# The filter of a spectral layer in another SBUF layout, and four more buffers for row results

## Chip, core and metric

The kernel runs on one core of one Trainium2 chip. The metric is the device time of one execution in microseconds. Before the change three runs took 368.7, 370.02 and 371.12 us, so the median is 370.02 us.

## What is computed

A layer in two halves, its output, and the gradients of its inputs:

```python
def _A_ref(x, w_r, w_i):                       # x: 2048 x 448
    X = rfft2(x.astype(float32), axes=(-2, -1))  # 2048 x 225, complex
    X = X * (w_r + 1j * w_i)                     # the filter: two planes of 2048 x 225, bf16
    return irfft2(X, s=(S, D), axes=(-2, -1)).astype(bfloat16)

def _B_ref(x, w1, b1, w2, b2):
    h = _layernorm(x, axis=-1)
    u = gelu(einsum("bsd,sf->bdf", h, w1) + b1)  # f = 1792
    y = einsum("bdf,fs->bds", u, w2) + b2
    return y.transpose(0, 2, 1)

h  = x + _A_ref(_layernorm(x), A_w_r, A_w_i)
h2 = h + _B_ref(_layernorm(h), B_w1, B_b1, B_w2, B_b2)
# returned: h2, and the gradients for x, A_w_r, A_w_i, w1, b1, w2, b2 under grad_out
```

All inputs and outputs are bf16. The gradients of A_w_r and A_w_i have the shape of the filter, 2048 x 225 each.

## The kernel before

The Fourier transform of the 448 columns and of the 2048 rows is done with matmuls. The 2048 rows are split into 16 x 128.

**Forward rows** (up to 45 us). For each of 16 groups of 128 rows, `row_a` and `row_b` make a short transform along the rows and the transform along the columns on TensorE (PE). `row_b` evicts its result from PSUM into a buffer of `cs_ring`; when both halves of a buffer are full, `defer` plans a reshuffle: a DMA on the queue of SyncE (SP) from the buffer, SBUF to SBUF, into `D2` (region r2). There are eight such reshuffles (line 669) and, before the change, four buffers in region r452, so the fifth to eighth buffer fill waits until an earlier reshuffle has read its buffer.

**Beside it.** While the row groups run, `fill(n)` puts matmuls of another product in between: 14 blocks of 16 matmuls that need w2 transposed. `load_w2T` (line 306) loads those blocks with DMA transposes on the SP queue. The filter is loaded in the same loop: `w_io` is a generator that issues one DMA per step, and `W_AT` says how many steps each of the 16 loop turns takes. Tables of sines that the mixing needs (`Ut`, `Vt`, from `base` and `gen_UV`) are made on VectorE (DVE), GpSimd (POOL) and ScalarE (ACT) at the same time.

**Mixing** (`s2_stage`, forward from 61 us). Four sets of four groups. For each set, small 32 x 32 matmuls (`four`, line 223) on `D2` finish the row transform; the results are evicted to `x`, which is `Xs` in region rX; `w_mult` multiplies by the filter on DVE in complex arithmetic, two groups at a time: two large products (128 x 904) and two sums (128 x 452) each. Then `four` again mixes back, and 32 more reshuffles (line 698) bring the result to `D3`. Between the sets `fill` puts in the other product's matmuls. `inv_rows` then finishes the inverse transform.

**The rest.** From 117 us on come the two large products of the second half, and then the gradients. The backward pass repeats rows, mixing and inverse rows. In its mixing (264 to 318 us) `bwd_mult` does `w_mult`, and then with `Xs` the gradient of the filter, which overwrites the filter in region rW. The inverse rows of the backward pass (from 318 us) are woven with matmuls of the weight gradients. `w_io` issues the filter's gradients as stores there, in the turns that `GW_AT` names.

**What sets the order.** PE, DVE, ACT and SP keep the order in which the program issues the work. Evictions go to ACT or DVE: `evac` compares two running sums of estimated costs, and `Meter.slack` limits how far the sums may drift apart (2.0, in the backward mixing 10.0). `defer` puts a DMA into SP's order at a planned time after PE's matmuls.

**The filter's layout.** Region rW holds `W` as [128 partitions, 16 groups, 2 planes, 226]; 225 columns are used, the last is set to zero. Partition 32i + c*16 + l (i, c, l from 0 to 3, 1 and 15) holds row 16i + g + 128l for c = 0, and the mirrored row 128 - 16i - g + 128l for c = 1; g is the group. The loads go per plane and per i: one move for c = 0, one for c = 1, and one for a single row that falls out of the pattern. That makes 18 moves, each to 16 neighbouring partitions, in runs of 450 bytes:

```python
for p0, g0, g1, row, dims in ((0, 0, 16, 16 * i, [[DF, 16], [1, DF]]),
                              (16, 0 if i else 1, 16, 128 - 16 * i - (not i), [[-DF, 16 if i else 15], [1, DF]]),
                              (16, 0, 1, 64, [[1, DF]])):
```

Of the kernel before, what the change touches and what calls it, by code (L numbers as in the profile page):

```python
# [12 lines left out]
I32 = mybir.dt.int32  # L13
ALU = mybir.AluOpType
# [108 lines left out]
def kernel(  # L123
# [339 lines left out]
    def gen_UV():  # L463
        i_, c_, s_ = decode(gp_)
        nrow, i16, z, mk, k0, k1, ou, ov0, ov1, pu, pv = (col() for _ in range(11))
        gp_madd(nrow, c_, 16.0, s_)
        gp_.tensor_scalar(out=i16, in0=i_, scalar1=16.0, scalar2=None, op0=ALU.mult)
        gp_.tensor_scalar(out=z, in0=i_, scalar1=0.0, scalar2=None, op0=ALU.is_equal)
        gp_.tensor_tensor(out=mk, in0=z, in1=c_, op=ALU.mult)
        gp_.tensor_scalar(out=k1, in0=mk, scalar1=-1.0, scalar2=1.0, op0=ALU.mult, op1=ALU.add)  # L470
        gp_.tensor_tensor(out=k0, in0=k1, in1=z, op=ALU.add)
        gp_.tensor_scalar(out=k0, in0=k0, scalar1=-1.0, scalar2=2.0, op0=ALU.mult, op1=ALU.add)
        gp_.tensor_scalar(out=ou, in0=c_, scalar1=1536.0, scalar2=1536.0, op0=ALU.mult, op1=ALU.add)
        gp_.tensor_scalar(out=ov0, in0=c_, scalar1=-512.0, scalar2=2048.0, op0=ALU.mult, op1=ALU.add)
        gp_.tensor_scalar(out=ov1, in0=ov0, scalar1=1024.0, scalar2=None, op0=ALU.add)
        for pt, o, kk in ((pu, ou, -1536.0), (pv, ov1, -512.0)):
            gp_.tensor_scalar(out=pt, in0=s_, scalar1=64.0, scalar2=kk, op0=ALU.mult, op1=ALU.add)
            gp_madd(pt, pt, mk, o)
        yield
        ve.tensor_scalar(out=permI[:], in0=krow[:, 0:32], scalar1=nrow, scalar2=None, op0=ALU.is_equal)  # L480
        ve.scalar_tensor_tensor(out=base[:, 0, 1, :], in0=fix, scalar=mk, in1=base[:, 0, 1, :], op0=ALU.mult, op1=ALU.add)
        bi = base.bitcast(I32)
        ve.tensor_scalar(out=bi, in0=base, scalar1=i16, scalar2=None, op0=ALU.add)
        ve.tensor_scalar(out=bi, in0=bi, scalar1=2047 - 64, scalar2=None, op0=ALU.bitwise_and)
        yield
        for dst, o0, o1, pt in ((Ut, ou, ou, pu), (Vt, ov0, ov1, pv)):
            t = ftmp(1024 if dst is Ut else 2048, 16, 2, 16).bitcast(I32)
            for k, o in ((0, o0), (1, o1)):
                ve.tensor_scalar(out=t[:, :, k, :], in0=bi[:, :, k, :], scalar1=s_, scalar2=o, op0=ALU.mult, op1=ALU.add)
                yield  # L490
            ve.tensor_scalar(out=t[:, 0, 1, :], in0=bi[:, 0, 1, :], scalar1=s_, scalar2=pt, op0=ALU.mult, op1=ALU.add)
# [3 lines left out]
            sc.activation(out=dst[:].rearrange("p g m -> p (g m)"), in_=t.rearrange("p g k l -> p (g k l)"), func=ACT.Sin,  # L495
                          scale=s2048, bias=half_uv)
            yield True
            for c, k in ((1, k0), (0, k1)):
                v = dst[:, 0, 16 * c:16 * c + 16]
# [55 lines left out]

    W = cut(rW, 0, NG, 2, KW)

    def w_io(dr, di, store):  # L560
        for c_, d in ((0, dr), (1, di)):
            for i in range(4):
                for p0, g0, g1, row, dims in ((0, 0, 16, 16 * i, [[DF, 16], [1, DF]]),
                                              (16, 0 if i else 1, 16, 128 - 16 * i - (not i), [[-DF, 16 if i else 15], [1, DF]]),
                                              (16, 0, 1, 64, [[1, DF]])):
                    if i and row == 64 and g1 == 1:
                        continue
                    p0 += 32 * i
                    sb = W[p0:p0 + 16, g0:g1, c_, 0:DF]
                    d_ap = bass.AP(d.tensor, d.offset + row * DF, [[P * DF, 16]] + dims)  # L570
                    nc.sync.dma_start(out=d_ap if store else sb, in_=sb if store else d_ap)  # L571
                    yield

    r452_ring = ring(r452, 0, 8, 2, KW)
    Xs = cut(rX, 0, NG, 2, KW)
# [2 lines left out]
    Y_ring = ring(rS, 1808, 2, 4, 2, KW)  # L578
    aT_ring = ring(rAT, 0, 2, 4, P)
    D2 = cut(r2, 0, NG, 2, KW)  # L580
    cs_ring = ring(r452, 0, 4, 2, 2, KW)
    D3 = cut(r3, 0, NT, 2, KW)

    _ei = [0]

    def resh_eng():
        _ei[0] += 1
        return nc.sync

    def rowbase(s_):  # L590
        return 32 * (s_ // 4) + s_ % 4
# [54 lines left out]
    def row_b(h, quarters=False):  # L646
# [19 lines left out]
        else:  # L666
            evac(out=cs[:, c], in_=pv)
        if c:
            defer(RESH_LAG, lambda: nc.sync.dma_start(out=D2[u:u + 125:4, 8 * e:8 * e + 8].rearrange("p g c k -> p (g c k)"),
                                                      in_=cs.rearrange("p x c k -> p (x c k)")), cs)  # L670

    def s2_stage(get_x, on_mult, n1, n2, gap, after=None, scale=None):
# [15 lines left out]
        for s in range(5):  # L688
            if s < 4:
                x = get_x(s)  # L690
                for a, pv in enumerate(four((Vt, Ut, Un), s, 1, lambda a, g, r: D2[blk(r), g])):
                    evac(out=x[:, a], in_=pv, scale=scale)
            fill(n1)
            if s:
                for g, pv in zip(set_groups(s - 1), four((VTt, UTt, UTn), s - 1, -1, lambda a, g, r: y[blk(r), a])):
                    ab = r452_ring.next()
                    evac(out=ab, in_=pv)
                    defer(RESH_LAG, lambda g=g, ab=ab: nc.sync.dma_start(out=D3[rowbase(g):rowbase(g) + 29:4, :, :, :], in_=ab), ab)
# [10 lines left out]
        ve.tensor_scalar(out=dst, in0=src, scalar1=-1.0, scalar2=None, op0=ALU.mult)  # L709

    def w_mult(xc, w, y, conj):
        wr = w[:, :, 0:1, :].broadcast_to([P, 2, 2, KW])
        wi = w[:, :, 1:2, :].broadcast_to([P, 2, 2, KW])
        p1, p2 = p_ring.next(), p_ring.next()
        ve.tensor_tensor(out=p1, in0=xc, in1=wr, op=ALU.mult)
        ve.tensor_tensor(out=p2, in0=xc, in1=wi, op=ALU.mult)
        ve.tensor_tensor(out=y[:, :, 1, :], in0=p1[:, :, 0, :], in1=p2[:, :, 1, :],
# [103 lines left out]
    base = ftmp(3072, 16, 2, 16)  # L821
    fix = ftmp(3584, 16)
    pcolb = col()
    ve.tensor_copy(out=pcolb, in_=pcol)
    nc.vector.memset(base[:, 0, 0, 0:1], 0.0)
    nc.vector.memset(base[:, 0, 1, 0:1], 0.0)
    for k in range(2):
        gp_.iota(base.rearrange("p (e a c) k l -> p k e a c l", e=2, a=4)[:, k],
                 pattern=[[8, 2], [18, 4], [1, 2], [128 - 256 * k, 16]], base=1920 * k,
                 channel_multiplier=0, allow_small_or_imprecise_dtypes=True)  # L830
    gp_.iota(fix, pattern=[[256, 16]], base=-1920, channel_multiplier=0, allow_small_or_imprecise_dtypes=True)
# [380 lines left out]


    def bwd_mult(s, j, xc, y):
        xs = set_of(Xs, s)[:, 2 * j:2 * j + 2]
        gw = set_of(W, s)[:, 2 * j:2 * j + 2]
        w_mult(xc, gw, y, True)
        p1, p2 = p_ring.next(), p_ring.next()
        ve.tensor_tensor(out=p1, in0=xc, in1=xs[:, :, 0:1, :].broadcast_to([P, 2, 2, KW]), op=ALU.mult)
        ve.tensor_tensor(out=p2, in0=xc, in1=xs[:, :, 1:2, :].broadcast_to([P, 2, 2, KW]), op=ALU.mult)  # L1220
        ve.tensor_tensor(out=gw[:, :, 0, :], in0=p1[:, :, 0, :], in1=p2[:, :, 1, :], op=ALU.add)
        ve.tensor_tensor(out=gw[:, :, 1, :], in0=p1[:, :, 1, :], in1=p2[:, :, 0, :], op=ALU.subtract)

# [65 lines left out]
            fill(8)  # L1289
        rows(t)  # L1290
    fill(N_FILL_B[2])
    Meter.slack = 10.0
    s2_stage(lambda s: X_ring.next(), bwd_mult, 14, 22, N_FILL_B[4], {1: lambda: load_du(0), 3: lambda: load_du(2)},
             2.0 * INV_SD)
    Meter.slack = 2.0
    g_out = w_io(out_2, out_3, True)
    X_AT = {0: 2, 4: 3}
    GW_AT = tuple(range(14)) + (1, 3, 5, 7)

    def gx_consumer(t, py):  # L1300
        if t in X_AT:
# [90 lines left out]
```

## Time and profile before

The profiled execution took 368.8 us; its span, from the first to the last instruction, is 367.0 us.

| | busy us | share of the span |
|---|---|---|
| PE, matmuls | 334.0 | 91% |
| PEld, weight loads (beside PE) | 174.7 | 48% |
| DVE | 248.2 | 68% |
| ACT | 198.3 | 54% |
| POOL | 69.0 | 19% |
| SP's DMA queue, share of 16 engines | | 87.2% |

| stretch, us | what runs | PE busy, us | DMA, GB/s |
|---|---|---|---|
| 0 to 21 | loads, tables | 14.5 of 21.0 | 250 |
| 21 to 45.6 | forward rows, filter loads | 23.0 of 24.6 | 166 |
| 45.6 to 61.1 | up to the first mixing matmul | 3.3 of 15.5 | 158 |
| 61.1 to 98.2 | forward mixing | 35.3 of 37.1 | 170 |
| 98.2 to 117.2 | inverse rows | 18.3 of 19.0 | 241 |
| 117.2 to 264.7 | large products, backward rows | 145.3 of 147.5 | 210 |
| 264.7 to 318 | backward mixing | 51.5 of 53.3 | 233 |
| 318 to 367 | inverse rows, weight gradients, stores | 42.8 of 49.0 | 244 |

How to read the views: the slices cut the span into 40 equal parts of 9.2 us, each digit is a busy share in tenths, and PEclk is the clock that was granted to PE. The chain of waits follows the work back from the last instruction, in order of time, as start, length and what; `SPq` is an instruction that issues a DMA, and `DMA a<-b` the time until such a move arrived. The waits list an engine, the line and tile, and what ended its idle time. In the groups of instructions each line has the operation, the tiles, the shape, the count, the busy time and the mean time of one in ns, and the idle time before. Names such as `r` stand for regions whose number is left out. Line 82 is a helper through which all DVE and ACT work goes, and line 218 the one through which most matmuls go.

### The profile page before, as it was taken

The page shows a single profiled execution, that of the slowest core. Times are in us where ns is not written, and L with a number is a line of the kernel's source. Part 1 is how long each engine was busy: PE and PEld are TensorE (multiplying, and loading weights), DVE is VectorE, ACT ScalarE, POOL GpSimd, SP SyncE. Part 2 cuts the span into 40 slices and gives each one's busy share as a digit, 9 for nine tenths or more (in the row PEclk, how much of TensorE's full clock was granted, in tenths as well). Part 3 has the DMA queues.
Part 4 walks back from the last instruction along what each step waited for, and adds up shares of the span by engine and source line. Part 5 has one row for each costly group of instructions (what it writes and reads, how often), then busy time and mean ns, then how long its engine had stood idle before and what let it go on. Part 6 is the DMA issues. An engine that isn't in the chain of part 4 may idle for free.

```text
span 367.0 us, 7798 instructions
## 1 busy us (share of the span) xinstructions
PE 334.0 (91%) x2810; PEld 174.7 (48%) x2819; DVE 248.2 (68%) x662; ACT 198.3 (54%) x436; POOL 69.0 (19%) x220
## 2 busy tenths in 40 slices
PE   8769833998999999999999999999898999999993
PEld 3346511444564555555555555554333434456551
DVE  8896323685188488859423788887389585479993
ACT  5466331364298645451321245557358887479972
POOL 5766000000022000000100111110000000047981
PEclk9989965999999999999999999999999999999999
DMA  8999999656994899967786898855986698999987
GB/s 222 275 191 162 178 146 181 150 122 167 263 319 167 284 327 290 261 164 211 208 195 159 176 204 162 194 93 138 293 267 192 206 242 232 225 282 239 212 242 262
DMA packets 151087, 78.03 MB, mean 213 GB/s; under 512 B 99784, under 2 KB 144072, under 8 KB 150920
## 3 DMA queue, kind: packets, MB, share of 16 engines
q1 hardware_dynamic: 150760, 77.13, 87.2%
q8 instruction: 22, 0.36, 0.4%
q10 hardware_dynamic: 288, 0.39, 0.3%
q14 instruction: 17, 0.14, 0.1%
HBM read 25.71 MB, written 22.04 MB: 130 GB/s over the span
## 4 chain that ended last, share of the span: by engine, by line
PE 72%; DVE 7%; DMA 6%; SPq 5%; ACT 5%; issue 2%; DVEq 0%; POOL 0%; ACTq 0%
PE ps_mm L218 62%; PE ps_ff L218 8%; DVE r L82 3%; DMA r<-r 3%; PE ps_ff L223 3%; SPq L306 3%; ACT rO L82 2%; DVE rS L82 2%; DMA rW<-in_A_w_i_dram 2%; DMA rA<-in_A_x_dram 1%; ACT r L82 1%; DVE rA L82 1%; SPq L316 1%; ACT rX L82 0%; SPq L571 0%
## 5 line engine op out<-in xcount | busy, mean ns | idle before, releaser
L218 PEld LDWEIGHTS <-r 128*128 128x128 bf16 (+2 forms) x600 | 56.0, 105 | 44.9 <-issue 2.3
L218 PEld LDWEIGHTS <-rS 128*128 128x128 bf16 (+2 forms) x496 | 40.3, 98 | 40.7 <-issue 8.1
L218 PE MATMUL ps_mm<-rD,r 128*128 128x448 bf16 x224 | 44.5, 352 | 0.0
L82 ACT CAST rO<-ps_mm 128x512 bf16<-128x512 f32 (+1 forms) x67 | 35.9, 586 | 13.3 <-PE ps_mm L218 8.8
L218 PEld LDWEIGHTS <-rst 128*128 128x128 bf16 (+1 forms) x320 | 23.4, 97 | 31.5 <-issue 14.6
L218 PE MATMUL ps_mm<-rC,rE 128*128 128x448 bf16 x144 | 34.9, 382 | 1.1 <-DMA rC<-in_grad_out_dram 1.0
L82 ACT CAST r<-ps_ff 128x452 bf16<-128x452 f32 x47 | 25.6, 585 | 18.5 <-DMA r<-r 10.8
L218 PE MATMUL ps_mm<-rB,r 128*128 128x448 bf16 x160 | 31.2, 352 | 0.1
L218 PE MATMUL ps_mm<-rG,rst 128*128 128x512 bf16 (+1 forms) x122 | 26.7, 380 | 0.9 <-ACT rO L82 0.4
L218 PE MATMUL ps_mm<-r,rst 128*128 128x512 bf16 (+2 forms) x144 | 27.2, 345 | 0.2 <-ACT rG L82 0.2
L82 DVE CAST r<-ps_ff 128x452 bf16<-128x452 f32 x17 | 10.4, 634 | 21.1 <-DMA r<-r 13.2
L82 ACT ACTIVATE r<-ps_mm,rstd_h 128x448 bf16<-128x448 f32 x16 | 10.2, 635 | 26.8 <-PE ps_mm L218 26.8
L82 DVE SCALAR_TENSOR_TENSOR r<-ps_mm,b2col,r 128x448 bf16<-128x448 f32 x16 | 10.9, 683 | 19.9 <-PE ps_mm L218 17.2
L82 ACT ACTIVATE r<-rC 128x448 bf16<-128x448 bf16 x16 | 9.1, 572 | 26.6 <-DMA out_dram<-r 18.7
L218 PE MATMUL ps_mm<-rE,rS 128*128 128x448 bf16 x112 | 21.5, 352 | 0.0
L82 ACT ACTIVATE rG<-rG 128x896 bf16<-128x896 bf16 x14 | 13.3, 951 | 14.9 <-DVE rG L82 14.7
L218 PEld LDWEIGHTS <-rO 128*128 128x128 bf16 (+1 forms) x165 | 15.2, 98 | 12.3 <-ACT rO L82 0.2
L82 ACT CAST rS<-ps_ff 128x512 bf16<-128x512 f32 x31 | 17.9, 582 | 5.0 <-PE ps_ff L218 4.9
L1137 POOL TENSOR_SCALAR lcol<-lcol 128x1 f32<-128x1 f32 x16 | 8.5, 530 | 64.7 <-ACT r L82 64.7
L218 PEld LDWEIGHTS <-rE 128*128 128x128 bf16 x144 | 14.3, 104 | 12.9 <-issue 4.4
L82 ACT CAST rG<-ps_mm 128x512 bf16<-128x512 f32 (+1 forms) x34 | 16.7, 543 | 6.7 <-PE ps_mm L218 6.4
L218 PE MATMUL ps_ff<-csI,rAT 113*128 113x224 bf16 (+1 forms) x108 | 19.0, 298 | 0.6 <-ACT rAT L82 0.4
(191 smaller groups left out, 604.5 us busy)
## 6 DMA issues: line engine op xcount, KB each, us to landing
out_dram<-rO SPq DMA_DIRECT2D x34, 256.0 KB
r<-in_B_w_dram SPq DMA_DIRECT2D x5, 1024.0 KB
r<-r SPq DMA_DIRECT2D x16, 226.0 KB
r<-r SPq DMA_DIRECT2D x32, 113.0 KB
rS<-in_B_w_dram SPq DMA_DIRECT2D x4, 896.0 KB
out_dram<-rG SPq DMA_DIRECT2D x10, 256.0 KB
rO<-in_B_w_dram SPq DMA_DIRECT2D x2, 1024.0 KB
rC<-in_grad_out_dram SPq DMA_DIRECT2D x4, 448.0 KB
```

The costliest lines, as they stand in the source:

```text
L82: fn(**kw)
L218: nc.tensor.matmul(out, lhsT=lhsT, rhs=rhs, start=start, stop=stop)
L223: nc.tensor.matmul(out, lhsT=lhsT, rhs=rhs, start=start, stop=stop)
L306: nc.sync.dma_start_transpose(out=wT, in_=B_w2[j * P:(j + 1) * P, :].rearrange("f (t c) -> f t c", c=P))
L316: nc.sync.dma_start(out=go_tp[:, 4 * q:4 * q + 4, :], in_=go_tp_d[:, 4 * q:4 * q + 4, :])
L1137: gp_.tensor_scalar(out=m1, in0=ms, scalar1=-1.0 / D, scalar2=None, op0=ALU.mult)
```

## The change

The filter is kept plane by plane: [128 partitions, 2 planes, 16 groups, 225], without the padding column. The two kinds of rows now alternate over the partitions: partition 32i + 2l + c instead of 32i + 16c + l. In an even partition the 16 groups of a plane are then one run of 7200 bytes in SBUF and in memory, and one move brings all 64 even partitions of a plane. The mirrored rows stay runs of 450 bytes, 16 partitions per move, but these lie two apart, over 32. Loads and stores go from 18 to 12 moves each. The tables `Ut` and `Vt` follow the new order of partitions, so their intermediate steps are made with another stride. DVE's products take 225 columns instead of 226. `cs_ring` gets four more buffers, in region rX, for the forward rows alone. The filter's moves are issued in other loop turns, and `Meter.slack` in the backward mixing goes from 10.0 to 7.0.

```diff
-        ve.scalar_tensor_tensor(out=base[:, 0, 1, :], in0=fix, scalar=mk, in1=base[:, 0, 1, :], op0=ALU.mult, op1=ALU.add)
+        ve.scalar_tensor_tensor(out=base[:, 0, :, 1], in0=fix, scalar=mk, in1=base[:, 0, :, 1], op0=ALU.mult, op1=ALU.add)
...
-            t = ftmp(1024 if dst is Ut else 2048, 16, 2, 16).bitcast(I32)
+            t = ftmp(1024 if dst is Ut else 2048, 16, 16, 2).bitcast(I32)
             for k, o in ((0, o0), (1, o1)):
-                ve.tensor_scalar(out=t[:, :, k, :], in0=bi[:, :, k, :], scalar1=s_, scalar2=o, op0=ALU.mult, op1=ALU.add)
+                ve.tensor_scalar(out=t[:, :, :, k], in0=bi[:, :, :, k], scalar1=s_, scalar2=o, op0=ALU.mult, op1=ALU.add)
...
-    W = cut(rW, 0, NG, 2, KW)
+    Wc = cut(rW, 0, 2, NG, DF)
+    W = Wc.rearrange("p c g k -> p g c k")
 
     def w_io(dr, di, store):
+        Wq = Wc.rearrange("(q s) c g k -> s q c g k", s=2)
         for c_, d in ((0, dr), (1, di)):
+            moves = [(Wq[0][:, c_].rearrange("q g k -> q (g k)"), 0, [[16 * DF, 4], [P * DF, 16], [1, 16 * DF]])]
             for i in range(4):
-                for p0, g0, g1, row, dims in ((0, 0, 16, 16 * i, [[DF, 16], [1, DF]]),
-                                              (16, 0 if i else 1, 16, 128 - 16 * i - (not i), [[-DF, 16 if i else 15], [1, DF]]),
-                                              (16, 0, 1, 64, [[1, DF]])):
-                    if i and row == 64 and g1 == 1:
-                        continue
-                    p0 += 32 * i
-                    sb = W[p0:p0 + 16, g0:g1, c_, 0:DF]
-                    d_ap = bass.AP(d.tensor, d.offset + row * DF, [[P * DF, 16]] + dims)
-                    nc.sync.dma_start(out=d_ap if store else sb, in_=sb if store else d_ap)
-                    yield
+                g0 = 0 if i else 1
+                moves.append((Wq[1][16 * i:16 * i + 16, c_, g0:NG, :], P - 16 * i - g0,
+                              [[P * DF, 16], [-DF, NG - g0], [1, DF]]))
+            moves.append((Wq[1][0:16, c_, 0, :], 64, [[P * DF, 16], [1, DF]]))
+            for sb, row, dims in moves:
+                d_ap = bass.AP(d.tensor, d.offset + row * DF, dims)
+                nc.sync.dma_start(out=d_ap if store else sb, in_=sb if store else d_ap)
+                yield
...
-    cs_ring = ring(r452, 0, 4, 2, 2, KW)
+    cs_ring = Ring(ring(r452, 0, 4, 2, 2, KW).views + ring(rX, 512, 4, 2, 2, KW).views)
...
     def w_mult(xc, w, y, conj):
-        wr = w[:, :, 0:1, :].broadcast_to([P, 2, 2, KW])
-        wi = w[:, :, 1:2, :].broadcast_to([P, 2, 2, KW])
-        p1, p2 = p_ring.next(), p_ring.next()
+        wr = w[:, :, 0:1, :].broadcast_to([P, 2, 2, DF])
+        wi = w[:, :, 1:2, :].broadcast_to([P, 2, 2, DF])
+        p1, p2 = (p_ring.next()[:, :, :, 0:DF] for _ in range(2))
+        xc, y = xc[:, :, :, 0:DF], y[:, :, :, 0:DF]
...
-    gp_.memset(W[:, :, :, DF:KW], 0.0)
...
-    W_AT = {t: 1 if t < 14 else 2 for t in range(NT)}
+    W_AT = {t: 1 for t in range(1, 13)}
...
+    del cs_ring.views[4:]
+    cs_ring.i = 0
...
     def bwd_mult(s, j, xc, y):
-        xs = set_of(Xs, s)[:, 2 * j:2 * j + 2]
+        xs = set_of(Xs, s)[:, 2 * j:2 * j + 2, :, 0:DF]
...
-    Meter.slack = 10.0
+    Meter.slack = 7.0
...
-    GW_AT = tuple(range(14)) + (1, 3, 5, 7)
+    GW_AT = tuple(range(12))
```

More of the change, by code (lines that the diff above doesn't have):

```diff
@@ L486, in gen_UV @@
         for dst, o0, o1, pt in ((Ut, ou, ou, pu), (Vt, ov0, ov1, pv)):
-            t = ftmp(1024 if dst is Ut else 2048, 16, 2, 16).bitcast(I32)
+            t = ftmp(1024 if dst is Ut else 2048, 16, 16, 2).bitcast(I32)
             for k, o in ((0, o0), (1, o1)):
-                ve.tensor_scalar(out=t[:, :, k, :], in0=bi[:, :, k, :], scalar1=s_, scalar2=o, op0=ALU.mult, op1=ALU.add)
+                ve.tensor_scalar(out=t[:, :, :, k], in0=bi[:, :, :, k], scalar1=s_, scalar2=o, op0=ALU.mult, op1=ALU.add)
                 yield
-            ve.tensor_scalar(out=t[:, 0, 1, :], in0=bi[:, 0, 1, :], scalar1=s_, scalar2=pt, op0=ALU.mult, op1=ALU.add)
+            ve.tensor_scalar(out=t[:, 0, :, 1], in0=bi[:, 0, :, 1], scalar1=s_, scalar2=pt, op0=ALU.mult, op1=ALU.add)
             ve.tensor_scalar(out=t, in0=t, scalar1=2047, scalar2=None, op0=ALU.bitwise_and)
@@ L494, in gen_UV @@
             yield True
-            sc.activation(out=dst[:].rearrange("p g m -> p (g m)"), in_=t.rearrange("p g k l -> p (g k l)"), func=ACT.Sin,
+            sc.activation(out=dst[:].rearrange("p g m -> p (g m)"), in_=t.rearrange("p g l k -> p (g l k)"), func=ACT.Sin,
                           scale=s2048, bias=half_uv)
@@ L498, in gen_UV @@
             for c, k in ((1, k0), (0, k1)):
-                v = dst[:, 0, 16 * c:16 * c + 16]
+                v = dst[:, 0, :].rearrange("p (l k) -> p k l", k=2)[:, c]
                 ve.tensor_scalar(out=v, in0=v, scalar1=k, scalar2=None, op0=ALU.mult)
@@ L580 @@
     D2 = cut(r2, 0, NG, 2, KW)
-    cs_ring = ring(r452, 0, 4, 2, 2, KW)
+    cs_ring = Ring(ring(r452, 0, 4, 2, 2, KW).views + ring(rX, 512, 4, 2, 2, KW).views)
     D3 = cut(r3, 0, NT, 2, KW)
[L584 to L588, printed above, removed]
+    resh = [nc.sync]
     def rowbase(s_):
@@ L668, in row_b @@
         if c:
-            defer(RESH_LAG, lambda: nc.sync.dma_start(out=D2[u:u + 125:4, 8 * e:8 * e + 8].rearrange("p g c k -> p (g c k)"),
+            defer(RESH_LAG, lambda: resh[0].dma_start(out=D2[u:u + 125:4, 8 * e:8 * e + 8].rearrange("p g c k -> p (g c k)"),
                                                       in_=cs.rearrange("p x c k -> p (x c k)")), cs)
@@ L697, in s2_stage @@
                     evac(out=ab, in_=pv)
-                    defer(RESH_LAG, lambda g=g, ab=ab: nc.sync.dma_start(out=D3[rowbase(g):rowbase(g) + 29:4, :, :, :], in_=ab), ab)
+                    defer(RESH_LAG, lambda g=g, ab=ab: resh[0].dma_start(out=D3[rowbase(g):rowbase(g) + 29:4, :, :, :], in_=ab), ab)
             if s < 4:
@@ L820 @@
     sc.activation(out=warm, in_=eps_x, func=ACT.Sqrt)
-    base = ftmp(3072, 16, 2, 16)
+    base = ftmp(3072, 16, 16, 2)
     fix = ftmp(3584, 16)
@@ L824 @@
     ve.tensor_copy(out=pcolb, in_=pcol)
-    nc.vector.memset(base[:, 0, 0, 0:1], 0.0)
-    nc.vector.memset(base[:, 0, 1, 0:1], 0.0)
+    nc.vector.memset(base[:, 0, 0, :], 0.0)
     for k in range(2):
-        gp_.iota(base.rearrange("p (e a c) k l -> p k e a c l", e=2, a=4)[:, k],
+        gp_.iota(base.rearrange("p (e a c) l k -> p k e a c l", e=2, a=4)[:, k],
                  pattern=[[8, 2], [18, 4], [1, 2], [128 - 256 * k, 16]], base=1920 * k,
@@ L1214, in bwd_mult @@
     def bwd_mult(s, j, xc, y):
-        xs = set_of(Xs, s)[:, 2 * j:2 * j + 2]
+        xs = set_of(Xs, s)[:, 2 * j:2 * j + 2, :, 0:DF]
         gw = set_of(W, s)[:, 2 * j:2 * j + 2]
         w_mult(xc, gw, y, True)
-        p1, p2 = p_ring.next(), p_ring.next()
-        ve.tensor_tensor(out=p1, in0=xc, in1=xs[:, :, 0:1, :].broadcast_to([P, 2, 2, KW]), op=ALU.mult)
-        ve.tensor_tensor(out=p2, in0=xc, in1=xs[:, :, 1:2, :].broadcast_to([P, 2, 2, KW]), op=ALU.mult)
+        xc = xc[:, :, :, 0:DF]
+        p1, p2 = (p_ring.next()[:, :, :, 0:DF] for _ in range(2))
+        ve.tensor_tensor(out=p1, in0=xc, in1=xs[:, :, 0:1, :].broadcast_to([P, 2, 2, DF]), op=ALU.mult)
+        ve.tensor_tensor(out=p2, in0=xc, in1=xs[:, :, 1:2, :].broadcast_to([P, 2, 2, DF]), op=ALU.mult)
         ve.tensor_tensor(out=gw[:, :, 0, :], in0=p1[:, :, 0, :], in1=p2[:, :, 1, :], op=ALU.add)
```

## The prediction

> **What bounds the kernel now.** First the page's slices: TensorE (PE) is busy nearly everywhere, with one hole in slices 5 and 6 (46 to 64 us), where its granted clock falls as well, while the DMA engines are full.
>
> ```profile
> PE   8769833998999999999999999999898999999993
> PEclk9989965999999999999999999999999999999999
> DMA  8999999656994899967786898855986698999987
> ```
>
> Then the table by stretches (stretch, length, busy us of PE, PEld, DVE, ACT, POOL, clock, DMA share, GB/s):
>
> ```profile
> 45.60:61.10 15.50, 3.30 (x16) 1.86 (x15) 2.91 (x10) 3.48 (x11) 0.11 (x1) 0.58 1.17 158
> 61.10:98.20 37.10, 35.29 (x521) 17.74 (x522) 21.10 (x43) 15.27 (x31) 0.67 (x2) 0.94 0.72 170
> 264.70:318.00 53.30, 51.45 (x613) 21.49 (x621) 37.70 (x77) 37.80 (x76) 0.00 (x0) 1.00 0.79 233
> ```
>
> Before 61.1 PE works 3.3 of 15.5 us: 12.2 us lie idle. The two mixing stages (second and third line) leave it 1.8 and 1.9 us. Only the hole can pay much. PE's waits (14 to 120 us) and the chain of waits say what ends it:
>
> ```profile
> PE ps_ff L223 <- DMA r<-r: 7.5, 1, 7.5
> PE ps_ff L545 <- ACT r L82: 4.7, 1, 4.7
> ```
>
> ```profile
> 46.92 0.58 SPq L571
> 47.55 5.90 DMA rW<-in_A_w_i_dram
> 53.52 7.53 DMA r<-r
> 61.10 1.21 PE ps_ff L223 x40
> ```
>
> The first mixing matmul (L223) waits for the seventh of eight reshuffles (r<-r, L669). SP issues that at 53.52, just after the filter load issued at 47.55 has arrived (53.45 by the trace's semaphore updates), and it arrives at 61.05. From 48 us on SP has eight moves outstanding: each issue follows the arrival of the eighth move before it (49.64 after 49.63, 51.41 after 51.35, 55.35 after 55.28). So the hole is a backlog of moves, and filter loads make up much of it; the moves from 15 to 62 us:
>
> ```profile
> DMA packets 19731, 8.18 MB, mean 174 GB/s; under 512 B 18445, under 2 KB 19469, under 8 KB 19725
> ...
> r<-r SPq DMA_DIRECT2D x8, 226.0 KB
> rW<-in_A_w_r_dram SPq DMA_DIRECT2D x7, 112.5 KB
> rW<-in_A_w_i_dram SPq DMA_DIRECT2D x7, 112.5 KB
> ```
>
> 4096 of the small packets are filter rows of 450 bytes.
>
> **The change, part by part.** (1) **Filter loads.** Per plane, four moves of 256 packets of 450 B become one of 64 packets of 7200 B; the four mirrored ones keep their packets. What the long ones cost depends on how many of the 16 DMA engines share them. The trace has moves that don't use all: the 32 with 8 partitions on one side (L698) post 9 arrivals on their semaphore, those with 16, 32 or 128 post 16. So the number of engines follows the outer count of a side, and the long move has an outer count of 4 in memory (4 blocks of 16 rows). I take 4 engines, which by that row is nearest, and keep 16 as the other end.
>
> The Trainium skill (DMA: Bandwidth & Descriptors, section "Why a DMA increments its semaphore by 16 and not by 1") says that a move is split over the largest number up to 16 that divides the slowest dimension of both sides; that speaks against this change, since 4 and 64 give 4 engines. The 9 arrivals agree with it (8 engines, and one write of the rest); by the page the sum is the 4-engine one below, with 16 engines this part would bring -8.4 us.
>
> The queue of the busiest engine, from the arrival at 22.8 us, ahead of which no filter packet stands, to the seventh reshuffle at 61.05, is 38.2 us. In it, by packets per engine and their mean time in this window: 5 transposes of w2 x 128 x 28.6 ns = 18.3; 7 reshuffles x 8 x 198 ns = 11.1; 16 filter moves x 16 x 53 ns = 13.6; together 43.0, or 1.126 times the time that passed, as packets overlap. With 4 engines the filter's 13.6 becomes 8 x 16 x 53 ns = 6.8 plus 2 x 16 x 307 ns = 9.8 (the 7168 B packets of the second load of grad_out): 46.0 / 1.126 = 40.9, which is 2.7 us **later**. That is the upper end: all packets stay as crowded as now. The lower end has each at its uncrowded time (medians: 256 B 18 ns, 1808 B 75 ns between 262 and 318 us, 450 B 26 ns, 7168 B 274 ns): 11.5 + 4.2 + 3.3 + 8.8 = 27.8, arrival at 50.6, 10.4 us **earlier**. Crowding does fall: all filter loads now stand ahead of the fifth reshuffle, and the last two reshuffles of the trace, with no filter move behind them in the way, arrived 0.24 and 0.61 us after the move before, against 1.2 to 1.8 us for the earlier ones. The mirrored rows lie over 32 partitions instead of 16. But the long moves stand right ahead of transposes. I take the middle, arrival at 57.1: **-3.9 us**.
>
> Does that reach the end? PE's order behind L223 is fixed; the two transposes that it needs next arrived at 63.6 and 65.8 and are read from 74.1 on, and they are issued after the reshuffles, so they come earlier too. From there to 350 us PE is the chain, and the row work behind it on DVE starts from PE's results. I count it in full.
>
> (2) **Eight buffers for row results.** They remove ACT's wait of 8.7 us and DVE's of 4.6 on old reshuffles, and PE's 4.7 us at L545. Alone this is worth nothing: PE then does its few remaining steps sooner and waits longer for the same reshuffle. It is needed for (1): row results end at 45.3 on PE, and with 0.6 for the eviction and 2.4 from issue to arrival (the uncrowded reshuffle at 246.1) 48.3 is the floor of the arrival. Added wait: buffers 5 to 8 lie in rX, which the first mixing results overwrite; ACT and DVE must wait for reshuffles 5 to 7 there, which PE awaits anyway. Nothing else is queued behind.
>
> (3) **SP.** Six filter loads fewer (some 0.5 us each) and none behind the fifth reshuffle, where the old order had five; the queue's backlog hides SP's time, so it is in (1). If the backlog were gone, SP would need 9 issues x 0.6 us from the third reshuffle to the seventh, 5 us, and set the pace.
>
> (4) **DVE products** on rows of 225 instead of 226, filter rows no longer starting on even places:
>
> ```profile
> L82 DVE TENSOR_TENSOR rS<-rC,rW 128x904 bf16<-128x904 bf16 x16 | 9.3, 625 | 0.5
> L82 DVE TENSOR_TENSOR rW<-rS 128x452 bf16<-128x452 bf16 x16 | 5.6, 392 | 0.3
> L82 DVE TENSOR_TENSOR r<-r 128x452 f32<-128x452 f32 x2 | 1.2, 622 | 0.0
> ```
>
> The first two give 0.52 ns per element and 0.157 us fixed, the f32 row 1.03 ns. No row has an odd length. Bounds: 0.62 and 0.39 us as now, or 1.08 and 0.62 at the f32 rate. I take the first, the row nearest in kind and size: 0.
>
> On this the skill disagrees with itself: VectorE: DVE Perf Modes (section "Mode 2×_1P") wants 4-byte alignment for two elements per cycle, the Vector Engine (DVE) Microarchitecture Reference (section "5.1 Performance modes") says that alignment makes no difference; no run here shows it yet. By the first the sum is the slower rival's below, by the second 0.
>
> (5) **The rest.** Tables with another stride: four int32 operations of 0.40 us on DVE, bounds 0 to twice that (1.6 us); DVE idles 4.6 us at 38 to 42 us, so 0. A POOL memset of 0.24 us at 2 us goes: 0. Slack 7 for 10: by the instruction order three evictions of 0.5 to 0.6 us go from ACT to DVE in the backward mixing, where DVE has 15.6 us free; PE loses 0.8 us to ACT's evictions there, I take -0.3 (bounds -0.8, +1). Filter stores: 12 for 18, again two on 4 engines: PE waits for no move after 265 us, and the last store is no filter's (issued at 362.2, arrived at 365.97): 0, bounds -1 and +2, if 16 x 0.274 = 4.4 us on four engines hold up the stores that free buffers.
>
> Sum: -3.9 - 0.3 = **-4.2 us**. The profiled execution took 368.8 (span 367.0), so 364.6; it lay 1.2 under the median of 370.0, and for a median run I say **365.8**.
>
> **Rivals.** *The backlog really halves* (all 16 engines share the long moves): crowded, 46.0 - 9.8 + 2 x 4 x 307 ns = 38.7, over 1.126, arrival at 57.1; uncrowded it meets the floor of 48.3. Middle 52.7, -8.4 - 0.3: 361.3. For it: the gaps of 0.24 and 0.61 us; against: the 9 arrivals. *The backlog stays*, the change doesn't do what it says: four engines carry what sixteen did, arrival between 60 and 63.8, about +1: 371. For it: transposes need all engines, so SP is held by the slowest. *Slower: DVE falls to one element per cycle.* Per set forward 4 x 0.46 + 4 x 0.23 = 2.8 us more, backward twice that, 5.5. Sets follow each other every 5.6 us forward with DVE busy 5.3, and every 10.2 backward with 7.9 of products: 0.3 and 2.3 are free, so 4 x 2.5 + 4 x 3.2 = 23 us: 365.8 + 23 = 389. It decides from where the products lose 4.2 us in all: 4 x (2.8x - 0.3) + 4 x (5.5x - 2.3) = 4.2 at x = 0.44, a large product of about 0.82 us. Against it: only the length is new.
>
> **How the numbers follow.** Forecast 0.50, halved backlog 0.18, backlog stays 0.20, DVE 0.12. The range reaches from the first rival's early side (359, 2.3 below its middle) to the second's late end (370.0 + 2.7, 373 rounded) and leaves out the DVE case and little else. A change under 1% (3.7 us) can't be told from none here. Faster: 0.34 of the forecast's 0.50 and 0.18, 0.52. Same: 0.16 and 0.13 of the stayed backlog, 0.29. Slower: 0.07 and 0.12, 0.19.
>
> **What the new profile would show.** Right: PE's wait on r<-r at L223 ends near 57, no wait on ACT at L545, the long filter loads arrive with 5 updates on their semaphore and some 4.4 us after their start, products near 0.62 and 0.39 us. Wrong: 16 updates (then more is gained), the wait ending at 61 or later, products near 1.08, or new waits of evictions on stores after 320 us.

## The result and the profile after

| | kernel before | changed kernel |
|---|---|---|
| median of 20 executions | 370.02 us (368.19 to 374.21) | 369.06 us (363.81 to 373.46) |
| ratio of the times | | 0.9909, 95% interval 0.9881 to 0.9938 |
| profiled execution, its span | 368.8, 367.0 us | 368.16, 366.3 us |

The ratio leaves out executions more than 1.5% above their kernel's fastest (one of the kernel before, ten of the changed one, 369.8 to 373.5 us); it gives 3.4 us less time, the medians of all twenty 1.0 us less. The forecast was 365.8 us, 4.2 us less, in a range of 359 to 373.

The slices of the changed kernel's page: the hole from 46 to 64 us is still there (a 0 and a 7, where the kernel before had 3 and 3), and a second one has appeared near the end (the 6, 339 to 348 us).

```profile
PE   8679907989999999999999999999799999999694
PEclk9989977999999999999999999999999999999988
DMA  8999889767994999788776889839959699999784
```

The waits of PE in the changed kernel (total, times, longest, in us):

```profile
PE ps_ff L223 <- DMA r<-rX: 10.8, 1, 10.8
PE ps_ff L218 <- DVE r L82: 3.3, 1, 3.3
```

The wait of 7.5 us for the reshuffle and the one of 4.7 at L545 have become one of 10.8. It ends earlier, as the chain of waits of the changed kernel shows (start, us, what). The seventh reshuffle is issued at 54.69 and is in at 56.97. Ahead of it SP is the chain: the transposing load of w2 (L306) that it had issued at 42.62, shortly behind the second long filter load, held it for 6.6 us, until 49.21 (the chain counts it from 46.36 on), and nine moves followed at some 0.65 us each, the seventh reshuffle last. The long load, issued at 41.23, was in at 49.12:

```profile
46.36 2.85 SPq L306
49.21 0.05 issue
49.31 0.59 SPq L667
...
52.60 0.62 SPq L572
53.33 0.58 SPq L667
54.01 0.58 SPq L667
54.69 2.28 DMA r<-rX
56.97 0.14 issue
57.11 1.22 PE ps_ff L223 x40
```

L223 starts at 57.11 instead of 61.10, and the lead of 4.0 us is kept: 4.6 us at the first large product of the MLP's weights (112.59 against 117.20), still 4.6 at 231, 4.1 at the first L223 of the backward mixing (260.59 against 264.66), and 4.95 at the end of the backward mixing (313.01 against 317.96). But the span is only 0.7 us shorter. The table by stretches of the changed kernel (stretch, length, busy us of PE, PEld, DVE, ACT, POOL, clock, DMA share, GB/s), with the first mixing, the backward mixing and the tail, and under it the tail of the kernel before:

```profile
45.60:61.10 15.50, 4.74 (x66) 2.67 (x65) 4.52 (x14) 2.79 (x10) 0.00 (x0) 0.67 0.98 211
260.60:313.00 52.40, 51.11 (x612) 21.49 (x620) 40.33 (x82) 35.86 (x71) 0.00 (x0) 1.00 0.84 241
313.00:366.30 53.30, 44.59 (x315) 24.46 (x312) 39.53 (x118) 34.89 (x90) 24.14 (x64) 0.94 0.84 220
```

```profile
318.00:367.00 49.00, 42.77 (x314) 23.71 (x311) 39.38 (x118) 34.84 (x90) 28.64 (x64) 0.99 0.90 244
```

The same work at the end (315 and 314 recorded matmuls) takes 53.3 us instead of 49.0: TensorE idles 8.7 us in it instead of 6.2, and is busy 1.8 us longer at a granted clock of 0.94 instead of 0.99. The changed kernel's chain through this stretch shows what it stood for, and VectorE's waits agree:

```profile
334.50 0.17 DVE r L82
334.67 9.86 DMA out_dram<-r
...
344.65 1.13 DVE r L82 x3
345.78 0.04 issue
345.82 0.38 PE ps_ff L218 x4
```

```profile
DVE r L82 <- DMA out_dram<-r: 4.4, 1, 4.4
```

A store of two row tiles of gx (L1340), issued at 334.67, is in only at 344.53. Until then VectorE can't write the next rows into that buffer, and TensorE waits 3.3 us for VectorE. The store stands right behind the filter's second long store, which SP issued at 333.96 and which arrived at 343.97 with five updates on its semaphore. Of the sixteen updates of the store behind it, twelve came by 337.80, and the last four from 342.33 to 344.53, among those of the long one (four from 341.76 to 343.97). In the kernel before, the stores of L1340 that were issued up to 354 us arrived 3 to 5 us after their issue.

The products of VectorE after the change:

```profile
L82 DVE TENSOR_TENSOR rS<-rC,rW 128x900 bf16<-128x900 bf16 x16 | 9.4, 628 | 0.4
L82 DVE TENSOR_TENSOR rS<-rS 128x450 bf16<-128x450 bf16 x32 | 11.2, 395 | 0.6
L82 DVE TENSOR_TENSOR rW<-rS 128x450 bf16<-128x450 bf16 x16 | 5.6, 393 | 0.3
```

They took 625 and 392 ns on rows of 226; rows of 225 that start on odd places cost the same.

### The profile page after: what moved, and what is told of

Same layout as the page of the kernel before. It is cut to its first block, busy times and chain, and to the rows that moved or that the text cites. A ratio compares the mean times of both kernels' runs of the same rounds, so it can differ in the third digit from the quotient of the medians.

```text
span 366.3 us, 7779 instructions
## 1 busy us (share of the span) xinstructions
PE 332.6 (91%) x2810; PEld 174.2 (48%) x2819; DVE 251.1 (69%) x666; ACT 196.6 (54%) x431; POOL 64.0 (17%) x219
## 4 chain that ended last, share of the span: by engine, by line
PE 70%; DVE 9%; SPq 6%; DMA 6%; ACT 4%; issue 3%; POOL 0%; DVEq 0%; ACTq 0%
PE ps_mm L218 59%; PE ps_ff L218 7%; DVE r L82 5%; SPq L306 3%; PE ps_ff L223 3%; DVE rS L82 3%; DMA out_dram<-r 3%; ACT rO L82 2%; DMA rE<-in_A_x_dram 1%; DMA rA<-in_A_x_dram 1%; DVE rA L82 1%; SPq L667 1%; SPq L572 1%; DMA r<-rX 1%; SPq L316 1%
## 5 line engine op out<-in xcount | busy, mean ns | idle before, releaser
L218 PEld LDWEIGHTS <-r 128*128 128x128 bf16 (+2 forms) x600 | 56.3, 105 | 48.3 <-issue 5.7
L218 PE MATMUL ps_mm<-rC,rE 128*128 128x448 bf16 x144 | 33.1, 367 | 2.0 <-DMA rC<-in_grad_out_dram 1.9
L218 PE MATMUL ps_mm<-r,rst 128*128 128x512 bf16 (+2 forms) x144 | 28.1, 354 | 0.0
L82 ACT CAST r<-ps_ff 128x452 bf16<-128x452 f32 x41 | 22.6, 588 | 8.3 <-PE ps_ff L223 6.0
L82 ACT CAST rAT<-ps_ff 113x512 bf16<-113x512 f32 x24 | 14.0, 591 | 10.7 <-PE ps_ff L218 10.6
```

The lines of the kernel that those rows point to most:

```text
L82: fn(**kw)
L218: nc.tensor.matmul(out, lhsT=lhsT, rhs=rhs, start=start, stop=stop)
```

## Experiments

The theory after these traces: the loads brought what was forecast, and the long stores on four engines gave most of it back. Its rivals: the end is lost to something else (slack, order of evictions), or the wait is an accident of one execution. For the loads it was open what the remaining hole of 11 us consists of: the four engines, the number of moves, or the work of all 16 engines.

In the table, the seventh reshuffle is the move that the first L223 waits for; its times are those of SP's issue and of the last update on its semaphore, in the profiled execution.

| kernel | seventh reshuffle issued, in | ratio, interval | median (of) and the median before beside it |
|---|---|---|---|
| before | 53.5, 61.1 | 1 | |
| changed | 54.7, 57.0 | 0.991 (0.988 to 0.994) | 369.1 (20), 370.0 |
| e1 changed again | 55.7, 58.1 | 0.991 (0.987 to 0.995) | 370.1 (12), 371.5 |
| e2 stores on 16 engines | 56.3, 58.7 | 0.988 (0.984 to 0.992) | 366.2 (6), 371.5 |
| e3 loads on 16 engines | 52.4, 56.5 | 0.996 (0.993 to 0.999) | 369.5 (12), 371.5 |
| e4 both on 16 engines | 52.2, 56.3 | 0.979 (0.976 to 0.983) | 363.1 (6), 371.5 |
| e5 as e4, one transpose later | 48.2, 50.5 | 0.9705 (0.966 to 0.975) | 359.2 (6), 369.8 |
| e6 as e4, two transposes later | 45.1, 47.7 | 0.968 (0.964 to 0.972) | 358.1 (6), 369.8 |
| e7 before with eight buffers | 53.7, 61.5 | 1.002 (0.998 to 1.005) | 370.6 (10), 369.8 |
| e8 changed with four buffers | 55.7, 59.3 | none | 372.7 (4), 369.8 |
| e9 as e2, one transpose later | 53.3, 57.1 | 0.985 (0.982 to 0.989) | 365.0 (6), 370.1 |
| e10 as e5, slack 10 | 47.9, 50.5 | 0.969 (0.965 to 0.973) | 359.0 (6), 370.1 |

### e1 to e4: which of the long moves matters

e1 is the changed kernel itself, beside the other three on the same chip. e2, e3 and e4 split the long moves; with the condition `store` for e2, `not store` for e3 and always for e4 (the lines of the condition are left out here), and with the 18 places that the moves had before the change:

```diff
-            moves = [(Wq[0][:, c_].rearrange("q g k -> q (g k)"), 0, [[16 * DF, 4], [P * DF, 16], [1, 16 * DF]])]
+            moves = []
             for i in range(4):
+                moves.append((Wq[0][16 * i:16 * i + 16, c_].rearrange("q g k -> q (g k)"), 16 * i,
+                              [[P * DF, 16], [1, 16 * DF]]))
```

> The changed kernel once more, beside the three that follow, on one chip. Theory (moves on four engines): time 0.991 of the kernel before (its interval was 0.988 to 0.994), some 366.7 us; the first reshuffles arrive at about 57 us and TensorE waits some 11 us for them; in the last 50 us a store of the row results lands some 10 us after its issue, behind the second long filter store, VectorE waits some 4 us for it and TensorE some 3 us. Rival (that last wait is an accident of one profiled execution): it is not there again, and the span is some 363 us.

> Only the filter's stores are changed: each long store of 64 partitions becomes four of 16 partitions, still in 7200-byte runs, so that each goes over 16 engines; 18 stores again in place of 12, at the places that they had before the change. Theory (the long stores on four engines hold up the stores behind them): no store of row results lags by more than some 6 us, TensorE's wait of 3.3 us near 345 us goes, and the time is 363 us (0.980 to 0.984 of the kernel before), some 3 to 4 us under the changed kernel. Rival (the time in the last 50 us is lost to the smaller slack or to the order of the evictions): no change, 366 to 367 us, 0.991. Rival (six more stores cost more than they free): 367 to 369 us.

> Only the filter's loads are changed: each long load becomes four of 16 partitions in 7200-byte runs over 16 engines, 18 loads at the places that they had before the change; the stores stay as in the changed kernel. Theory (the two long loads on four engines, 8.2 and 7.9 us from issue to arrival, hold the two transposing loads behind them on SP for 7.1 and 6.6 us): these come down to about 3 us each, the seventh reshuffle arrives 5 to 8 us earlier, at 49 to 52 us, and the time is 359 to 362 us (0.970 to 0.978). Rival (the backlog is set by the number of moves and the bytes, not by the engines): six more loads put the seventh reshuffle at 58 to 60 us and the time at 368 to 370 us. Rival (the hole is filled but its end then waits for SP's transposes): 364 us.

> Both: loads and stores of the filter's long half in 7200-byte runs over 16 engines. Theory: the two gains add up, 355 to 358 us (0.960 to 0.968 of the kernel before). Rival (number and bytes of the moves decide the loads, slack the end): 367 to 369 us (0.992 to 0.997). If the loads' gain is taken back later, as the changed kernel's was, 362 us.

**The stores.** e1's profiled execution came out as its rival had it: 365.1 us, span 363.3, and the wait at the end nearly absent. The second long store was issued at 332.82, 1.1 us earlier than in the changed kernel's first profile, and the store behind it was in at 342.65 instead of 344.53, while TensorE's own work stood 1.1 us later (the first matmuls behind the backward mixing start at 313.99 instead of 312.85). The two together are the 3.0 us by which the wait is shorter. The first line below is PE's only wait after 313 us in e1; the two stretches after it are from the changed kernel and from e2:

```profile
PE ps_ff L218 <- DVE r L82: 0.3, 1, 0.3
```

```profile
340.00:350.00 10.00, 6.72 (x45) 4.06 (x45) 5.58 (x18) 4.07 (x13) 4.52 (x12) 0.83 0.84 221
```

```profile
340.00:350.00 10.00, 10.00 (x75) 5.72 (x73) 9.64 (x32) 8.61 (x25) 8.41 (x18) 1.00 0.93 276
```

In e2 PE waits for nothing after 313 us, and no store of gx issued up to 347 us lags by more than 6.3 us. So the wait is not a fixed loss: it depends on where that store falls against the long one and against TensorE's work. e3 has it again (3.9 us, profiled execution 370.9 us), e4 does not. e3 and e4 differ in the stores alone, and there the time shows them: 0.996 to 0.979, 6.2 us, with intervals far apart. With the loads as changed, the ratios 0.991 and 0.988 overlap, so the time does not show a gain. e2 missed the 363 us of the theory: 366.2 us fits the rival (366 to 367) as well, and it is the trace of e2, without the wait, that speaks for the theory.

**The loads.** Here theory and first rival both failed. The rival's time came for e3 (368 to 370, measured 369.5), but not its arrival of 58 to 60, and e4 with the same loads takes 363.1 us: the time of e3 is that of its stores. e4 missed its 355 to 358 us too, since the loads had not brought the 5 to 8 us expected of them. On 16 engines the two transposing loads held SP for 3.9 and 2.2 us (e3) instead of 7.1 and 6.6, as the theory said. The seventh reshuffle was issued 2.3 us earlier than in the changed kernel and 4 us earlier than in e2. It arrived only 0.5 to 2.2 us earlier, though, because the reshuffles issued after 42 us now took 4.0 to 6.3 us to arrive instead of 2.4 to 3.7 (e2). e3 and e4 also keep the 18 moves and the loop turns of the kernel before. So their arrivals at 56.5 and 56.3, against 61.5 in e7 below, which has the eight buffers too, come from the new layout with its long runs, not from fewer moves or from the new turns. PE's wait for it in e3 and e4:

```profile
PE ps_ff L223 <- DMA r<-rX: 10.1, 1, 10.1
```

```profile
PE ps_ff L223 <- DMA r<-rX: 9.4, 1, 9.4
```

Between 22 and 45 us in e4 the 256-byte packets of the w2 transposes alone take 17.5 us on each of the 16 engines. That makes them the candidate for the next limit.

### e5, e6: the transposes that stand ahead of the reshuffles

```diff
-CAP = 8
+CAP = 7     # e5;  6 in e6: transposing loads of w2 issued ahead of the hole
```

> The kernel with all filter moves on 16 engines (363.1 us, 0.979 of the kernel before; seventh reshuffle in at 56.3 us), with one more of the transposing loads of w2 held back: the one that SP issued at 40.0 us comes behind the eighth reshuffle. Each such load fills 128 packets per engine. Theory (what is left of the hole is work of the DMA engines, most of it these transposes, 17.5 of the 23 us between 22 and 45 us): 128 packets x 18 to 28.6 ns = 2.3 to 3.7 us less ahead of the reshuffles, the seventh arrives at 52.6 to 54 us, the time falls by as much, to 359.4 to 360.8 us (0.969 to 0.973). Rival (SP's eight outstanding moves and their latency set the pace, not the engines' work): the seventh arrives at 55.5 to 56.3 us and the time stays at 362.5 to 363.5 us. Rival (the held load is then missed by the work that fills TensorE after the hole): the hole shrinks, but TensorE waits for rE near 66 us and the time is 363 us or more.

> The same with two transposing loads held back, those issued at 33.4 and 40.0 us. Theory: 4.6 to 7.4 us less ahead of the reshuffles, the seventh arrives at 49 to 52 us, near the floor of 48.3 us that the row results set; the time is 356 to 359 us (0.959 to 0.967), unless TensorE misses the second of the held loads, near 61 us, which would give back 1 to 3 us. Rival (outstanding moves set the pace): arrival not before 54.5 us, 362 us or more.

The transposes ahead of the reshuffles were the limit, and the rival with an arrival of 55.5 us or later is out. In e5 the seventh reshuffle arrived 5.8 us earlier, more than the 2.3 to 3.7 us of packets that were moved past it. The moved load had also held SP for 2.1 us in e4; the two together would make 4.4 to 5.8 us by estimate, but no run separates them. From the fifth reshuffle on, the lag behind an issue is 2.3 to 3.2 us again, and the chain of e5 now runs through SP's own issues, one move of 0.6 us after the other:

```profile
46.17 0.58 SPq L672
46.80 0.60 SPq L577
47.45 0.62 SPq L577
48.07 0.05 issue
48.18 2.32 DMA r<-rX
50.54 1.21 PE ps_ff L223 x38
```

In e6 the arrival is 2.8 us earlier still, but PE begins to miss what was moved (the third line below is a held transpose; waits of e6, 14 to 120 us), and the time can't be told from e5's:

```profile
PE ps_ff L218 <- DMA r<-r: 2.4, 1, 2.4
PE ps_ff L223 <- DMA r<-rX: 2.1, 1, 2.1
...
PE ps_mm L218 <- DMA rE<-in_B_w_dram: 0.9, 1, 0.9
```

Both are faster than either kernel, by about 3% of the time of the one before.

### e9: four engines for the loads, without the transpose behind them

Stores as in e2, loads as in the change, `CAP = 7` as in e5.

> The kernel with the filter's long loads on four engines as in the change, its stores on 16 engines (366.2 us, seventh reshuffle in at 58.7 us), and one transposing load of w2 held back behind the eighth reshuffle: the one that stood right behind the second long load and kept SP for 7.2 us. Theory (the four engines cost much only because a transposing load stands behind them and keeps SP until they are done): without it the reshuffles behind the second long load are issued from 43 to 48 us on, the seventh arrives at 50 to 52.5 us, 6 to 8 us earlier, and the time is 358.5 to 360.5 us, no worse than with 16 engines (359.2). Rival (only the engines' work counts): 2.3 to 3.7 us earlier, 55 to 56.4 us, and 362.5 to 364 us. Rival (the reshuffles must pass the four busy engines too, each move being done only when its last engine is): the third to fifth arrive at 50 to 52 us however early they are issued, and the seventh at 53 to 55 us, 361 to 363 us.

The theory fell. The last rival has the mechanism, though its times were too early; by number alone the first rival was nearer (55 to 56.4 us and 362.5 to 364; measured 57.1 and 365.0). With the transpose out of the way the third and fourth reshuffles were issued at 42.8 and 44.8, right behind the long load (41.3), and arrived at 53.2 and 54.7, 10 us later, after that load (51.7). The seven moves behind it, spread over all 16 engines, were done only after it, and their updates show why: of the third reshuffle's sixteen, twelve came from 46.8 to 47.7 and the last four from 51.8 to 53.2. Four of the engines were late, as many as the long load uses. And since eight moves were then outstanding, SP stood as well, from 46.7 to 51.8, until the long load was in; its waits (20 to 62 us) name it:

```profile
SPq L672 <- DMA rW<-in_A_w_i_dram: 5.0, 1, 5.0
```

So there are two limits one behind the other. With the transposes ahead, 16 engines for the loads bring 3.3 us (0.988 to 0.979, e2 and e4); with one transpose moved they bring 5.4 us (0.985 to 0.9705, e9 and e5). Moving the transpose alone brings 1.1 us, not to be told from nothing (e2 and e9, overlapping intervals); with 16 engines it brings 3.3 (e4 and e5).

### e7, e8: the eight buffers by themselves

```diff
-    cs_ring = ring(r452, 0, 4, 2, 2, KW)
+    cs_ring = Ring(ring(r452, 0, 4, 2, 2, KW).views + ring(rX, 512, 4, 2, 2, KW).views)
```

This in the kernel before is e7 (with the two lines that give the buffers back); the reverse in the changed kernel is e8.

> The kernel before with one part of the change alone: eight buffers for the forward row results in place of four. By the prediction nothing: the waits of ACT and VectorE for old reshuffles (8.7 and 4.6 us) and TensorE's 4.7 us at L545 go, but TensorE then waits longer for the same seventh reshuffle, which still arrives near 61 us; 370 to 371.5 us, 0.998 to 1.002. Rival (the reshuffles were issued late because their rows were evicted late): the seventh is issued 2 to 4 us earlier and the time falls by 1 to 4 us, to 0.989 to 0.997.

> The changed kernel without that part: four buffers for the forward row results. By the prediction the eight buffers are needed for the gain of the loads. In the changed kernel's trace the first four reshuffles arrived at 39.7, 44.2, 52.0 and 54.5 us, which is when the buffers would come free; with an eviction and 1.1 us of lag the seventh could still be issued near 54 us, as it was (54.7), and the eighth would slip from 55.4 to about 56.5 us. So 0 to +1.2 us on the arrival, and 0 to +1 us on the time against the changed kernel (0.990 to 0.997 of the kernel before). Rival (the evictions of old rows hold up the loads and moves behind them too): the waits of the kernel before come back in full, 4.7 us at L545, and the seventh arrives at 59 to 61 us, as before the change.

e7 came out as predicted, and PE's wait for the reshuffle shows why: the waits at L545 and on the four buffers are gone, and the wait for the reshuffle, in at 61.5, has grown to take their place.

```profile
PE ps_ff L223 <- DMA r<-rX: 16.0, 1, 16.0
```

In e8 PE's waits before 120 us show the old stall back, as its rival had it, with ACT waiting 13.5 and VectorE 17.2 us on old reshuffles:

```profile
PE ps_ff L545 <- ACT r L82: 6.8, 1, 6.8
PE ps_ff L223 <- DVE r L82: 3.4, 1, 3.4
```

The third reshuffle, whose buffer the seventh needs, was in only at 54.2; the seventh was issued at 55.7 and in at 59.3. That is 2.3 us later than in the changed kernel's first profile, but 1.2 us later than in e1 and 0.6 later than in e2, which have eight buffers and the same loads, and in e1 it was issued at 55.7 too. So e8 does not decide between the 0 to 1.2 us expected and the rival's 59 to 61. Its four times, from 363.3 to 375.6 us, are too few and too far apart for a ratio, and in its profiled execution PE waited 5.6 us at the end for the rows behind the late store as well. Whether the loads' gain needs the eight buffers stays open.

### e10: slack

```diff
-    Meter.slack = 7.0
+    Meter.slack = 10.0     # in the kernel of e5
```

> The kernel with all filter moves on 16 engines and one transposing load held back (359.2 us, 0.9705 of the kernel before), with the slack of the backward mixing put back from 7 to 10. By the prediction slack 7 is worth 0.3 us (bounds a loss of 1 and a gain of 0.8), so 359.5 us, 0.969 to 0.974, not to be told from no change; in the profile TensorE waits twice for ACT's evictions (0.8 us) between 255 and 310 us, where it waits once (0.4 us) with slack 7. Rival (slack 7 is worth the 0.9 us by which this stage was shorter in the changed kernel): 360.1 us.

The evictions moved as expected: TensorE's waits for ACT between 250 and 310 us were one of 0.4 us with slack 7 (e5), and here

```profile
PE ps_mm L218 <- ACT rO L82: 0.8, 2, 0.4
PE ps_mm L218 <- ACT rG L82: 0.2, 1, 0.2
```

The ratios 0.9705 and 0.969 are the same within their intervals. Slack is worth less than can be measured here. The end was not lost to it either: e2 keeps slack 7 and has no wait there.

## Why the prediction was right, and where it was not

The time lay in the range, and the forecast of 4.2 us less is near the 3.4 us of the ratio. By the prediction's own line of 1% (3.7 us) those 3.4 us count as no change, to which it gave 0.29, against 0.52 for a gain. The gain came from the step that was to bring it: the buffers alone bring nothing (e7), and slack nothing that can be measured (e10). But the way in which it came was only in part the one forecast, and one term failed that in the profiled execution took most of it back.

1. **The filter loads: the size was right, with luck; the mechanism only in part.** Forecast was an arrival of the seventh reshuffle at 57.1 and -3.9 us; measured were 56.97 and -4.0 at L223, then 58.1 and 58.7 in two more profiled executions with the same loads. The forecast is the middle of bounds 13 us apart, so coming within 0.2 us of it is luck. The bounds were not made alike either: the upper one is divided by 1.126 for the overlap of packets, the lower one is not (with it the arrival would be 47.5, under the floor of 48.3). The packet times of 28.6 and 53 ns are means from 15 to 62 us; in the window that the sum names they are 30.5 and 54.2. And of the earlier reshuffles one followed the move before it by 0.9 us, not 1.2 to 1.8.

   Four engines share each long load: five updates each, so the row of the 8-partition moves led the right way, and the rule of the Trainium skill that it was weighed against (DMA: Bandwidth & Descriptors, "Why a DMA increments its semaphore by 16 and not by 1") agrees with these five. The 4.4 us named as the sign of a long load was wrong: 8.2 and 7.9 us. Its packets took 347 ns on average, and 16 of them make 5.6 us; that the rest went to other moves' packets on the same four engines fits, but the trace does not tell packets by engine. Crowding fell in part: a 450-byte packet took 29.7 ns on average (53 before), a reshuffle's packet 88 ns (198 before), but a transpose's 256 bytes 28.7 ns as before (28.6), all between 15 and 62 us.

   What set the arrival was not the queue of the busiest engine, as the sum has it, but SP: a transposing load behind each long load held it until that load was in. In nine such pairs (two each in the changed kernel, e1, e2 and e8, one in e9) SP came free within 0.4 us of the long load's arrival, though the profile names PE for part of that time. This is what the rival with the backlog that stays says ("SP is held by the slowest"); its price of about +1 us was wrong, since the moves behind were quick again (the last four reshuffles 2.3 to 2.7 us).
2. **Eight buffers:** nothing alone, as forecast (e7), and no wait at L545 is left. That the loads' gain needs them is not shown (e8).
3. **SP:** the prediction held that its pace counts only once the backlog is gone, with 5 us from the third reshuffle to the seventh. The changed kernel is already that case: 49.31 to 54.69, 5.4 us. In e5 the chain runs through SP again.
4. **VectorE's products: right.** 0.63 and 0.39 us. Of the two rules of the Trainium skill that disagreed, this case's rows agree with the Vector Engine (DVE) Microarchitecture Reference ("5.1 Performance modes"), which says that alignment makes no difference.
5. **Slack:** -0.3 can't be resolved; e10 agrees with something that small.
6. **Filter stores: this term was mis-sized.** It stood at 0 with an upper bound of +2, "if 16 x 0.274 = 4.4 us on four engines hold up the stores that free buffers". That is the mechanism that came, with a price of 4.3 us in the profiled execution. The 4.4 us supposed that a long store has its engines to itself. The two took 10.2 and 10.0 us: their 16 packets per engine took 326 and 347 ns each on average, 5.2 and 5.6 us. In e1 these packets took 273 ns, 4.4 us as supposed, and the stores still 8.8 and 9.1 us; the rest fits the packets of the other outstanding moves on the same four engines. And the reason given for 0, that PE waits for no move after 265 us, was read from a kernel in which the stores there arrived in 2 to 5.6 us; how much later they may come before a buffer is missed was not worked out.

Of the **rivals**, the one with 16 engines was tried as e3 and e4. Its price was wrong: 52.7 was forecast for the arrival, 56.5 and 56.3 were measured. Ahead of the reshuffles stood the transposes (e5), and the moves took 4.0 to 6.3 us each; the sum of crowded packets gave 57.1 for that case, and was the better end. The arrival at 57 to 58.7 us lies ahead of the 60 to 63.8 of the backlog that stays, and VectorE did not slow down.

## What to carry to other kernels

Before a move is made longer, count how many DMA engines its outer dimension leaves it. The one on four of them here was late itself and held all seven moves that were issued within 4.8 us behind it (e9), so price such a move by the most urgent consumer among the moves behind it, and at its crowded time (here 8 to 11 us for 460 KB). Where several limits stand one behind the other, taking one away shows little: 16 engines for the loads, or one transpose moved, brought 0.9% and 0.3% each alone, and 1.8% together. Look for such a store's victims where buffers are few, at the end of a kernel as much as in the hole that the change was made for.

## What was not expected of the hardware

- A move on four engines took 8 to 11 us for 460 KB, where the filter's short loads of 112.5 KB on 16 engines took 2.9 to 4.5 us in the changed kernel when they did not stand right behind it. In e9 seven moves issued up to 4.8 us after it, spread over 16 engines, were all in only after it: 10 us from issue to arrival, with the last four of sixteen updates late.
- A transposing load issued within 1.6 us behind such a move kept SP for 7.1 and 6.6 us in the changed kernel, until the move was in; in e3 and e4 with no such move ahead it was 2 to 4 us.
- In two profiled executions of the same kernel the store behind the second long one was in at 344.5 and 342.7 us, with TensorE's own work 1.1 us earlier in the first. Its wait was 3.3 us in the one and 0.3 in the other, and the granted clock from 340 to 350 us 0.83 and 1.00: a loss that hangs on a microsecond or two of alignment.
